# Block attention and a routed expert layer on one core: the first unit's weight loads move to another queue, v is loaded six tiles ahead

## The chip, the cores and the metric

The kernel runs on one core of a Trainium2 chip. The metric is the device time of one execution in microseconds (us). TensorE does the matrix products and transposes, VectorE (DVE), ScalarE (ACT) and GpSimd (POOL) the element-wise work; SyncE (SP) only issues transfers (DMAs). GpSimd issues transfers too, on a queue of its own. All transfers are carried by the same 16 DMA engines.

## What is computed

Attention in blocks of 64 tokens, without any link between blocks, and then a layer of 16 experts in 4 groups, of which each token uses one:

```
# q, k, v: batch 8, heads 8, 576 tokens, 64 wide; blocks of 64 tokens
attn = softmax(q_c @ k_c^T / 8)          # 64 x 64 for each block and head
x = attn @ v_c                           # seen as 4608 tokens x 512
g = argmax(x @ w_group)                  # one of 4 groups
e = argmax(x @ w_expert[g])              # one of its 4 experts
out[token] = p(g) * p(e) * relu(x @ w1[g, e]) @ w2[g, e]
# w1: 16 x 512 x 1024, w2: 16 x 1024 x 512, all float32
```

## The kernel before

The 4608 tokens are 36 tiles of 128 (two blocks of 64 with all 8 heads). A first stage does attention and routing tile by tile; rows of x go to a buffer in HBM (`xs`), sorted by expert. A second stage, the critical block with loops at run time, takes units of up to 256 rows of one expert through w1 and w2. The change lies in the first stage.

**Order.** The order of TensorE, VectorE and ScalarE in the first stage is written out by hand; SyncE and GpSimd are not named in that clause. `HEAD` runs first, then one round for each t from 0 to 32, then `TAIL`, a long list for the last tiles. A word is a letter and a number: `Qn` (`load_qk`) loads q and k for two tiles, four transfers of 256 KB or more and smaller ones; `Vn` (`load_v`) loads v for one tile, 256 KB; `an` transposes q (even n) or k (odd n) of tile n // 2 on TensorE, with a copy on ScalarE; `b` is the scores of a tile (L277), `s` subtracts the maximum on VectorE, `e` the exponential on ScalarE, `c` transposes the probabilities on TensorE and copies them (`pT`) on ScalarE, `p` is the product with v (L313), `n` normalizes into x on VectorE (L330), `x` transposes x (TensorE, and a copy on ScalarE). Round t holds, in this order:

```
b(t) s(t) p(t-2) n(t-2)   a(2t+6)   c(t-1) e(t)   a(2t+7)   Q(t//2+4) if t is even   x(t-3)   load_v(t+4)   EXTRA[t]
```

`FIRST` stands in the place of the first `a` of round 0. After every four tiles the logits of that group of tiles are formed (`1`, L349, which reads the router's weights), transposed back (`2`) and ranked (`3`); VectorE's routing steps are spread between its other work by `more()`.

**Extras.** `EXTRA` puts further steps at the end of a round. `G0` (`load_wg`, L572) loads the router's weights, five small transfers by SyncE. `Z0` to `Z4` (`prefill`, L582) write zeros into parts of `xs` by SyncE. `F0` to `F5` (`first_loads`, L523) are for the first unit, whose expert `e0` VectorE chooses after 16 tiles: `F0` reads the number into a register and loads the first half of w1 (1 MB), `F1` the second half, `F2` and `F3` gather the unit's 256 rows, `F4` and `F5` load the halves of w2. Before, all of them are issued by GpSimd. `P0` to `P7` (`prep_static`, L192) split w1 into a high part (a copy on ScalarE, L197) and the rest (a subtraction on GpSimd, L198); P0, P1, P4 and P5 read the first half, the others the second. `X0` and `X1` (`first_x`) transpose the gathered rows. In `TAIL`, `W` copies w2's high part (L559, the first one shortly after the scores of tile 33), and `L` (`first_l1`) starts the first unit's first product. `R0` and `R1` load the next expert's w1 by SyncE into the same two buffers.

**Buffers.** The raw q and k have three buffers, v has eight (`NV`), the transposes share four PSUM tiles on their way to ScalarE. x of a group of four tiles has three buffers (`xl` and two of `xpool`); a buffer is written again when the rows of the group three before have been scattered to `xs` (L483, GpSimd). The scatter also waits for the zeros of `prefill`, which lie in the same buffer in HBM.

Of the kernel before, what the change touches and what calls it, by code (L numbers as in the profile page):

```python
# [27 lines left out]
E = G * EG  # L28
NT = N // P
# [11 lines left out]
NB0, NL0 = 2, 3  # L41
PB = 1

HEAD = "Q0 V0 Q1 V1 Q2 V2 V3 a0 a1"
FIRST = "a2 a3 Q3 a4 a5 a6"
EXTRA = {2: "G0", 4: "Z0", 5: "Z1", 6: "Z2", 7: "Z3", 8: "Z4",
         24: "F0", 26: "F1", 27: "F2 F3 P0", 28: "P1 P2", 29: "P3", 30: "P4 P5 F4", 31: "P6 X0", 32: "P7 X1 F5"}
TAIL = ("c32 m1 b33 m1 36 m1 s33 p31 b34 e33 W1 m4 x30 m1 n31 m3 s34 m1 L0 m1 e34 L1 c33 x31 b35 17 l7 m2"
# [43 lines left out]
def moe_kernel(tc, q, k, v, w_group, w_expert, w1, w2, cst, out):  # L92
    nc = tc.nc
    w1 = w1.rearrange("g e d f -> (g e) d f")
    w2 = w2.rearrange("g e f d -> (g e) f d")
    with ExitStack() as ctx:
# [24 lines left out]
        e0 = wpool.tile([1, 1], I32, name="e0")  # L121
# [22 lines left out]
        NP = 2  # L144
# [31 lines left out]
        def load1(eng, e, j):  # L176
            s = w1[e] if isinstance(e, int) else w1[ds(e, 1)].rearrange("o a b -> (o a) b")
            return eng.dma_start(w1r[j], s.rearrange("(c p) f -> p c f", p=P)[:, K1 * j:K1 * j + K1])

        def load2(eng, e, j):  # L180
            s = w2[e] if isinstance(e, int) else w2[ds(e, 1)].rearrange("o a b -> (o a) b")
            return eng.dma_start(w2r[j], s.rearrange("(c p) f -> p c f", p=P)[:, K2 * j:K2 * j + K2])
# [17 lines left out]
        with ExitStack() as c1:  # L200
# [24 lines left out]
            st, TL, FAST = {}, NT - 1, GL - 1  # L225

            def spans(c0, n):
                out, c = [], c0
                while c < c0 + n:
                    b, j = divmod(c, NCH)  # L230
                    m = min(c0 + n - c, NCH - j)
                    out.append((c - c0, m, b, j))
                    c += m
                return out
# [10 lines left out]
            def load_v(t):  # L245

                va = vbufs[t % NV]
                for i, m, b, j in spans(2 * t, 2):
                    nc.sync.dma_start(va[i * CH:(i + m) * CH, :, 0:HD], v[b, :, j * CH:(j + m) * CH, :].rearrange("h s d -> s h d"))
                st[t] = dict(va=va)  # L250
# [271 lines left out]

            def first_loads(i):  # L523
                if i == 0:
                    st["e0"] = nc.values_load(e0[0:1, 0:1], engines=[nc.gpsimd.engine], min_val=0, max_val=E - 1,
                                              skip_runtime_bounds_check_because=WHY)
                if i < NP:
                    load1(nc.gpsimd, st["e0"], i)
                elif i < NP + 2:
                    j = i - NP  # L530
                    r = nc.values_load(xi0[0:1, j:j + 1], engines=[nc.gpsimd.engine], min_val=0, max_val=E * RE * P,
                                       skip_runtime_bounds_check_because=WHY)
                    nc.gpsimd.dma_start(xg0[:, j, :], xs[ds(r, P), :])
                else:
                    load2(nc.gpsimd, st["e0"], i - NP - 2)

            def first_x(j):
                pt = ps_t.tile([P, 4, P], F32, name="tp")
# [27 lines left out]
            def more(n=1):  # L566

                for _ in range(n):
                    while routing and next(routing[0], True):
                        routing.pop(0)  # L570
# [8 lines left out]
            def last(t):  # L579
                return t >= 0 and t % NG == NG - 1  # L580
# [8 lines left out]
            def run(seq):  # L589
                g = dict(P=prep_static, X=first_x, L=first_l1, H=first_hi, D=first_lo, W=prep2_hi, w=prep2_lo, y=lambda i: prep2_lo(i, nc.vector), F=first_loads, R=reload, V=load_v,  # L590
                         Q=load_qk, G=load_wg, Z=prefill, a=stage_a)
                f = dict(b=stage_b, s=stage_sub, c=stage_ct, e=stage_exp, p=stage_pv, n=stage_norm, x=stage_xt)
                for z in seq.split():
                    if z[0] == "m":
                        more(int(z[1:]))
                    elif z[0] in g:
                        g[z[0]](int(z[1:]))
                    elif z[0] == "1":
                        stage_e1(int(z[1:]))
                    elif z[0] == "l":  # L600
                        stage_lts(int(z[1:]))
                    elif z[0] == "2":
                        stage_e2(int(z[1:]))
                    elif z[0] == "3":
                        stage_e3(int(z[1:]))
                    elif 0 <= int(z[1:]) < NT:
                        f[z[0]](int(z[1:]))

            with tc.manual_schedule(engines={mybir.EngineType.PE, mybir.EngineType.DVE, mybir.EngineType.Activation}):
                nc.sync.dma_start(cs[:, P:], cst[:, P:])  # L610
                run(HEAD)
                for t in range(TL - 2):
                    run("b%d s%d p%d n%d" % (t, t, t - 2, t - 2))
                    if last(t - 4):
                        run("1%d" % ((t - 4) // NG))
                    run("a%d" % (2 * t + 6) if t else FIRST)
                    if last(t - 4):
                        run("l%d" % ((t - 4) // NG))
                    if last(t - 7):
                        run("3%d" % ((t - 7) // NG))  # L620
                    more(2)
                    run("c%d e%d" % (t - 1, t))
                    run("a%d" % (2 * t + 7))
                    if t % 2 == 0 and t <= 26:
                        run("Q%d" % (t // 2 + 4))
                    run("x%d" % (t - 3))
                    if t + 4 < NT:
                        load_v(t + 4)
                    if last(t - 4):
                        run("2%d" % ((t - 4) // NG))  # L630
                    run(EXTRA.get(t, ""))
                run(TAIL)
# [751 lines left out]
```

## Time and profile before

| | |
|---|---|
| median of 3 runs | 685.59 us (681.66 to 689.75) |
| the profiled execution | 684.17 us |
| its span, from the first to the last instruction | 682.5 us |
| TensorE busy | 628.1 us (92%) |
| VectorE, ScalarE, GpSimd busy | 369.3, 293.3, 147.7 us |
| moved by DMA | 128.10 MB, 188 GB/s over the span |
| first stage | up to about 219 us |

The profile shows the profiled execution alone. Times in its views are counted from the first instruction. An engine counts as busy while it works, not while it waits for a semaphore; the "idle" of a row is the time just before its instructions, with what ended it behind the arrow. Line numbers (L277) are those of the kernel before. A DMA row by SPq or POOLq is the issue, not the transfer; the time to landing stands apart.

### The profile page before, as it was taken

Reading aid. Unit: us, or ns where it says so; the run is one execution under the profiler, and the core shown is the slowest. Engines: PE = TensorE matmul, PEld = TensorE weight load, DVE = VectorE, ACT = ScalarE, POOL = GpSimd, SP = SyncE. Lnnn points to the kernel's source line nnn. Section 1 sums busy time; section 2 is a strip of 40 time slices with the busy share of each in tenths; the row PEclk is TensorE's granted clock in tenths of the full one; section 3 lists DMA queues with packets and bytes.
Section 4 is the critical chain, followed back from the end, with each engine's and each line's share of the span. In section 5 each row is a group of like instructions: output and inputs, shape, how many; then the busy total and the mean of one; then the engine's idle time right before and its main releaser. Section 6 shows DMA issues by size and latency. Waiting matters only on the chain.

```text
span 682.5 us, 16774 instructions
## 1 busy us (share of the span) xinstructions
PE 628.1 (92%) x5866; PEld 558.9 (82%) x5867; DVE 369.3 (54%) x695; ACT 293.3 (43%) x418; POOL 147.7 (22%) x217
## 2 busy tenths in 40 slices
PE   5979789989587979999999999999999999999992
PEld 4868778877576778998988989998999998998981
DVE  1447566747458646722457776472721777854210
ACT  3545545657344243511438545251611465552110
POOL 1000222226325322022122411222111214222110
PEclk9889989989798979999999999999999999999996
DMA  9999999999932496831176984554441656931010
GB/s 190 208 174 213 246 222 236 221 257 261 263 122 79 150 370 234 300 121 59 57 260 212 335 331 176 168 207 139 165 151 61 259 218 235 335 129 64 21 45 15
DMA packets 151634, 128.10 MB, mean 188 GB/s; under 512 B 119006, under 2 KB 119262, under 8 KB 151584
## 3 DMA queue, kind: packets, MB, share of 16 engines
q1 hardware_dynamic: 140720, 93.76, 50.0%
q0 software_dynamic: 10864, 33.64, 14.1%
q8 instruction: 35, 0.57, 0.4%
q14 instruction: 15, 0.12, 0.1%
HBM read 106.23 MB, written 21.93 MB: 188 GB/s over the span
## 4 chain that ended last, share of the span: by engine, by line
PE 84%; issue 3%; DMA 3%; SPq 3%; DVE 3%; ACT 1%; POOLq 0%; DVEq 0%; ACTq 0%
PE py L827 27%; PE ph L812 18%; PE lgk L812 6%; PE ph L796 5%; PE o L313 5%; PE sc L277 5%; PE tp L259 5%; SPq L243 2%; PE tp L300 2%; PE tp L342 2%; DMA va<-in_v_dram 2%; PE py L844 2%; PE pxt L712 2%; PE lgk L349 1%; PE ph L758 1%
## 5 line engine op out<-in xcount | busy, mean ns | idle before, releaser
L812 PE MATMUL ph<-xt,w1h 128*128 128x256 f32 x672 | 100.4, 286 | 5.4 <-issue 5.4
L812 PEld LDWEIGHTS ph<-xt,w1h 128*128 128x128 f32 x672 | 91.0, 195 | 6.9 <-issue 5.9
L967 ACT ACTIVATE hth<-ph 128x512 fp32r<-128x512 f32 x43 | 25.7, 598 | 153.8 <-PE ph L812 150.6
L1295 POOL DMA_INDIRECT out_dram<-xl,io x37 | 41.6, 1124 | 166.2 <-DVE xl L1028 153.4
L1042 DVE TENSOR_TENSOR w2l<-w2r,w2h 128x1024 fp32r<-128x1024 f32 x60 | 69.5, 1218 | 6.5 <-ACT w2h L982 5.0
L1038 DVE TENSOR_TENSOR w1l<-w1r,w1h 128x2048 fp32r<-128x2048 f32 x28 | 63.0, 2289 | 13.2 <-ACT w1h L954 11.6
L827 PE MATMUL py<-w2h,hth 128*128 128x512 f32 x264 | 67.7, 398 | 0.0
L827 PE MATMUL py<-w2l,hth 128*128 128x512 f32 x264 | 65.3, 390 | 0.0
L827 PE MATMUL py<-w2h,htl 128*128 128x512 f32 x264 | 65.2, 389 | 0.0
L1028 DVE TENSOR_SCALAR xl<-py,io 128x512 f32<-128x512 f32 x33 | 24.7, 748 | 68.3 <-PE py L827 68.3
L285 DVE TENSOR_REDUCE m<-sc 128x8 f32<-128x512 f32 x36 | 24.8, 688 | 66.2 <-PE sc L277 66.1
L1061 DVE SCALAR_TENSOR_TENSOR htl<-ph,hth 128x512 fp32r<-128x512 f32 x40 | 27.4, 688 | 58.6 <-ACT hth L967 58.2
L827 PEld LDWEIGHTS py<-w2l,hth 128*128 128x128 f32 x264 | 49.6, 188 | 10.6
L827 PEld LDWEIGHTS py<-w2h,htl 128*128 128x128 f32 x264 | 49.6, 188 | 10.3
L259 PE MATMUL tp<-cs,qk 128*128 128x128 f32 x288 | 49.7, 302 | 8.1 <-DMA qk<-in_q_dram 6.9
L313 PE MATMUL o<-va,pT 64*64 64x65 f32 x1152 | 42.5, 225 | 14.8 <-DMA va<-in_v_dram 6.7
L827 PEld LDWEIGHTS py<-w2h,hth 128*128 128x128 f32 x264 | 47.6, 188 | 10.2 <-ACT hth L1013 0.9
L812 PE MATMUL ph<-xt,w1l 128*128 128x256 f32 x336 | 55.1, 286 | 0.5 <-DVE w1l L1038 0.5
L954 ACT CAST w1h<-w1r 128x2048 fp32r<-128x2048 f32 x28 | 52.2, 1905 | 4.1 <-DMA w1r<-in_moe_w_dram 2.1
L313 PEld LDWEIGHTS o<-va,pT 64*64 64x64 f32 x1152 | 39.0, 141 | 16.6 <-issue 13.5
L958 ACT CAST w2h<-w2r 128x2048 fp32r<-128x2048 f32 x28 | 52.3, 1928 | 0.0
L259 PEld LDWEIGHTS tp<-cs,qk 128*128 128x128 f32 x288 | 35.4, 153 | 18.6 <-issue 15.0
(259 smaller groups left out, 1057.5 us busy)
## 6 DMA issues: line engine op xcount, KB each, us to landing
w1r<-in_moe_w_dram SPq DMA_DIRECT2D x30, 1024.0 KB, 5.7
w2r<-in_moe_w_dram SPq DMA_DIRECT2D x30, 1024.0 KB, 7.3
xgr<-xs POOLq DMA_DIRECT2D x38, 257.0 KB, 5.6
qk<-in_q_dram SPq DMA_DIRECT2D x32, 256.0 KB, 5.5
qk<-in_k_dram SPq DMA_DIRECT2D x32, 256.0 KB, 5.8
va<-in_v_dram SPq DMA_DIRECT2D x32, 256.0 KB, 5.7
w1r<-in_moe_w_dram POOLq DMA_DIRECT2D x2, 1024.0 KB, 10.6
w2r<-in_moe_w_dram POOLq DMA_DIRECT2D x2, 1024.0 KB, 8.3
```

Source lines behind the costliest of these rows:

```text
L259: nc.tensor.transpose(pt[:, hp, :], st["q", t // 2][:, t % 2, z, 2 * hp:2 * hp + 2].rearrange("p h d -> p (h d)"), ident)
L277: nc.tensor.matmul(sc[HALF[x], hp, c], lhsT=st["T", u, 0][HALF[x], hp, k0:k0 + CH], rhs=st["T", u, 1][HALF[x], hp, k0:k0 + CH], start=True ...
L313: nc.tensor.matmul(o[HALF[c], x, hp * W:hp * W + W], lhsT=pT[HALF[c], hp, HALF[x]], rhs=s["va"][HALF[c], 2 * hp + x], start=True, stop=True)
L796: m = pe.matmul(ph[n], a_[:, c, 0:P], w_[:, c, n * 512:(n + 1) * 512], start=(i == 0), stop=(i == 11))
L812: m = pe.matmul(ph[f // 2][:, f % 2 * 256:f % 2 * 256 + 256], w_[:, c, f * P:(f + 1) * P], a_[:, c, :], start=(i == 0), stop=(i == 11))
L827: m = pe.matmul(py[j], a_[:, f, half[j]], w_(b, f), start=(i == 0), stop=(i == 23))
L954: lambda b, s, j: ac.copy(wt[b][0][:, s], w1r[j]), K1)
L958: lambda b, s, j: ac.copy(wt[b][2 + j], w2r[j]), K2)
L1038: lambda b, s, j: ve.tensor_sub(wt[b][1][:, s], w1r[j], wt[b][0][:, s].bitcast(F32)), K1, js)
L1042: m = ve.tensor_sub(wt[b][4 + 2 * j + i], w2r[j][:, 2 * i:2 * i + 2], wt[b][2 + j][:, 2 * i:2 * i + 2].bitcast(F32))
L1061: ve.scalar_tensor_tensor(out=htl()[:, 2 * b:2 * b + 2, :], in0=ph[b].rearrange("p (f t) -> p f t", f=2), scalar=0.0, in1=hth()[:, 2 * b:2 ...
L1295: gp.indirect_dma_start(out, bass.IndirectOffsetOnAxis(ap=io[:, j, 0:1].bitcast(I32), axis=0), yb[:, j, :], None, bounds_check=N - 1, oob_ ...
```

## The change

The loads of the first unit's w1 and w2 (`F0`, `F1`, `F4`, `F5`) are issued by SyncE, and SyncE reads `e0`; the gathers `F2` and `F3` stay with GpSimd. `F0` moves from round 24 to 26, `F1` from 26 to 27, `F5` from 32 to 31; `F2` and `F3` stay in round 27 and `F4` in round 30. `P0` to `P6` stand one round later than before, `P7` stays in round 32, `X0` and `X1` stay in rounds 31 and 32. v is loaded six tiles ahead of the round in place of four: `V3` leaves `HEAD`, `V3`, `V4` and `V5` enter `FIRST`, and each round loads v(t+6). `G0` moves from round 2 to round 1.

```diff
--- before.py
+++ after.py
@@ -41,10 +41,10 @@
 NB0, NL0 = 2, 3
 PB = 1
 
-HEAD = "Q0 V0 Q1 V1 Q2 V2 V3 a0 a1"
-FIRST = "a2 a3 Q3 a4 a5 a6"
-EXTRA = {2: "G0", 4: "Z0", 5: "Z1", 6: "Z2", 7: "Z3", 8: "Z4",
-         24: "F0", 26: "F1", 27: "F2 F3 P0", 28: "P1 P2", 29: "P3", 30: "P4 P5 F4", 31: "P6 X0", 32: "P7 X1 F5"}
+HEAD = "Q0 V0 Q1 V1 Q2 V2 a0 a1"
+FIRST = "a2 a3 Q3 V3 a4 V4 a5 V5 a6"
+EXTRA = {1: "G0", 4: "Z0", 5: "Z1", 6: "Z2", 7: "Z3", 8: "Z4",
+         26: "F0", 27: "F1 F2 F3", 28: "P0", 29: "P1 P2", 30: "P3 F4", 31: "P4 P5 X0 F5", 32: "P6 X1 P7"}
 TAIL = ("c32 m1 b33 m1 36 m1 s33 p31 b34 e33 W1 m4 x30 m1 n31 m3 s34 m1 L0 m1 e34 L1 c33 x31 b35 17 l7 m2"
         " p32 m2 s35 e35 c34 n32 27 m1 p33 m3 W2 c35 m1 p34 n33 W0 n34 m1 x32 W4 p35 m1 x34 x33 m4 n35 m3 x35"
         " m3 R1 m3 y0 H0 m1 W3 m1 37 18 l8 y1 m2 L2 m1 y2 m1 D0 m2 y3 m1 W7 W6 y4 m4 28 m6 L3 m5 W5 y5 H1 m2 L4"
@@ -522,17 +522,17 @@
 
             def first_loads(i):
                 if i == 0:
-                    st["e0"] = nc.values_load(e0[0:1, 0:1], engines=[nc.gpsimd.engine], min_val=0, max_val=E - 1,
+                    st["e0"] = nc.values_load(e0[0:1, 0:1], engines=[nc.sync.engine], min_val=0, max_val=E - 1,
                                               skip_runtime_bounds_check_because=WHY)
                 if i < NP:
-                    load1(nc.gpsimd, st["e0"], i)
+                    load1(nc.sync, st["e0"], i)
                 elif i < NP + 2:
                     j = i - NP
                     r = nc.values_load(xi0[0:1, j:j + 1], engines=[nc.gpsimd.engine], min_val=0, max_val=E * RE * P,
                                        skip_runtime_bounds_check_because=WHY)
                     nc.gpsimd.dma_start(xg0[:, j, :], xs[ds(r, P), :])
                 else:
-                    load2(nc.gpsimd, st["e0"], i - NP - 2)
+                    load2(nc.sync, st["e0"], i - NP - 2)
 
             def first_x(j):
                 pt = ps_t.tile([P, 4, P], F32, name="tp")
@@ -624,8 +624,8 @@
                     if t % 2 == 0 and t <= 26:
                         run("Q%d" % (t // 2 + 4))
                     run("x%d" % (t - 3))
-                    if t + 4 < NT:
-                        load_v(t + 4)
+                    if t + 6 < NT:
+                        load_v(t + 6)
                     if last(t - 4):
                         run("2%d" % ((t - 4) // NG))
                     run(EXTRA.get(t, ""))
```

## Rows read from the trace of the kernel before

**Rows 1.** The page: busy time of each engine (share of the span) and instructions.

```profile
PE 628.1 (92%) x5866; PEld 558.9 (82%) x5867; DVE 369.3 (54%) x695; ACT 293.3 (43%) x418; POOL 147.7 (22%) x217
```

**Rows 2.** Windows by stage: length, busy time by engine, TensorE's clock, DMA share, GB/s.

```profile
80.00:130.00 50.00, 43.05 (x768) 36.71 (x766) 28.83 (x105) 25.67 (x52) 10.76 (x15) 0.93 1.06 227
130.00:180.00 50.00, 41.39 (x739) 35.37 (x738) 28.97 (x92) 27.71 (x56) 23.74 (x26) 0.93 1.08 269
180.00:220.00 40.00, 32.81 (x441) 28.69 (x441) 26.01 (x85) 18.78 (x36) 12.62 (x13) 0.93 0.36 121
```

**Rows 3.** Waits of SyncE's queue, 0 to 181 us: total, times, longest.

```profile
SPq L243 <- PE sc L277: 3.0, 4, 1.0
```

**Rows 4.** Waits of TensorE, 20 to 181 us.

```profile
PE o L313 <- DMA va<-in_v_dram: 6.7, 2, 6.1
PE o L313 <- issue: 6.1, 1, 6.1
PE lgk L349 <- DMA wg<-in_moe_w_expert_dram: 3.6, 1, 3.6
```

**Rows 5.** The chain that ended last, 158 to 190 us: start, us, what.

```profile
164.06 13.66 DMA va<-in_v_dram
```

**Rows 6.** The page's DMA issues: count, size of one, median us to landing.

```profile
va<-in_v_dram SPq DMA_DIRECT2D x32, 256.0 KB, 5.7
```

**Rows 7.** TensorE in order of time, 156 to 216 us: start, us, instructions.

```profile
160.55 1.15 PE L313 MATMUL o<-va,pT 64*64 64x65 f32 x32 [0.53 <-DMA va<-in_v_dram]
...
170.57 1.15 PE L277 MATMUL sc<-kT,qT 64*64 64x64 f32 x32
177.85 2.00 PE L313 MATMUL o<-va,pT 64*64 64x65 f32 x32 [6.13 <-DMA va<-in_v_dram]
...
184.26 1.15 PE L277 MATMUL sc<-kT,qT 64*64 64x64 f32 x32
```

**Rows 8.** Windows of three stretches, columns as in rows 2.

```profile
100.00:110.00 10.00, 9.90 (x179) 8.44 (x179) 7.32 (x24) 5.60 (x12) 1.17 (x2) 1.00 0.94 204
...
176.90:183.70 6.80, 5.85 (x52) 5.76 (x53) 1.84 (x10) 2.39 (x5) 0.19 (x1) 0.50 0.95 217
250.00:255.00 5.00, 5.00 (x44) 5.00 (x44) 1.72 (x3) 3.29 (x3) 0.00 (x0) 1.00 1.05 396
```

**Rows 9.** SyncE's queue in order of time (four stretches): start, us of issuing, transfers.

```profile
69.80 1.04 SPq L584 DMA_DIRECT2D xs<-pad  x1
...
127.67 1.01 SPq L249 DMA_DIRECT2D va<-in_v_dram  x1
128.78 0.74 SPq L243 DMA_DIRECT2D qk<-in_q_dram  x1
...
164.06 16.64 SPq L249 DMA_DIRECT2D va<-in_v_dram  x7
...
167.38 5.60 SPq L249 DMA_DIRECT2D va<-in_v_dram  x2
```

**Rows 10.** GpSimd in order of time, with the issues of its transfers.

```profile
76.39 1.12 POOL L483 DMA_INDIRECT xs<-x,pos  x1 [71.78 <-DMA va<-in_v_dram]
...
133.01 0.79 POOL L178 DMA_DIRECT2D w1r<-in_moe_w_dram  x1
...
163.79 0.78 POOL L182 DMA_DIRECT2D w2r<-in_moe_w_dram  x1
164.58 1.32 POOL L198 TENSOR_TENSOR w1l<-w1r,w1h 128x512 fp32r<-128x512 f32 x1
```

**Rows 11.** ScalarE in order of time: copies of w1 and the first of w2.

```profile
152.04 0.66 ACT L197 CAST w1h<-w1r 128x512 fp32r<-128x512 f32 x1
...
157.13 1.17 ACT L197 CAST w1h<-w1r 128x512 fp32r<-128x512 f32 x2
...
188.34 0.60 ACT L559 CAST w2h<-w2r 128x512 fp32r<-128x512 f32 x1
```

**Rows 12.** VectorE in order of time: the first write into a used x buffer.

```profile
87.06 0.69 DVE L330 TENSOR_TENSOR x<-o,rc 128x512 f32<-128x512 f32 x1 [7.51 <-DMA xs<-x,pos]
```

**Rows 13.** Transfers into w1r: by SyncE (180 to 190 us), then by GpSimd (130 to 145 us).

```profile
DMA to landing us min/median/max: 4.8/5.9/6.9
DMA to landing us min/median/max: 9.4/10.6/11.8
```

## The prediction

> **What bounds the kernel now.** The engines' totals come first: TensorE is busy 92% of the span [rows 1], but that is a mean over two stages, and the change touches only the first. The windows by stage [rows 2] split them: from 80 to 180 us the DMA share stands at 1.06 and 1.08 while TensorE works 43.05 and 41.39 of 50 us; from 180 to 220 us the DMA share falls to 0.36. So I read the attention stage as bound by its transfers until the last v is in. The waits of SyncE's queue up to 181 us confirm it: the largest entry is 3.0 us in four waits [rows 3], and the seven entries add up to 10.8 us. The queue hardly waits for buffers; it hands out transfers as fast as the DMA engines take them, and each issue is held up by the transfers ahead of it. TensorE's own waits then show where a late transfer is met: 6.7 us for v, 6.1 us put down to "issue" (an x buffer, below), 3.6 us for the router's weights [rows 4]. The chain of waits gives the last gate: one v transfer (tile 30) took 13.66 us from issue to landing [rows 5], where 5.7 us is the median [rows 6]. TensorE's timeline shows what that does: scores of tile 32 at 170.57, then nothing until tile 30's value product at 177.85, and tile 33's scores at 184.26 [rows 7]. That last time, b33, is my yardstick: behind it the tail of the list and the routed stage run on as before, and what moves b33 moves the end.
>
> **The price of a transfer.** A 256 KB transfer of q, k or v costs 262144 B / 204 GB/s = 1.29 us, by the stretch 100 to 110 us, in which almost nothing else moves [rows 8]. From 128.78 us (Q15 is issued) to 167.38 + 5.60 = 172.98 us (v32 has been issued) [rows 9] the queue hands out Q15 to Q17 and v26 to v32, 12 + 7 = 19 such transfers, 24.4 of 44.2 us. The other 19.8 us went to GpSimd's queue beside it: four weight loads of 1 MB, the first issued at 133.01, the third at 163.79 [rows 10], two groups of scattered rows (2.1 MB) and two gathers (0.5 MB): 6.8 MB, or 345 GB/s. A weight load so costs 3.0 us of everybody's transfers; the ends are 2.65 (396 GB/s, 250 to 255 us [rows 8]) and 3.9 us (269 GB/s, 130 to 180 us [rows 2]).
>
> **The weights move to SyncE's queue.** At 128.78 the new order has handed out the same set as the old one (Q0 to Q14, v0 to v25). Up to the end of v32's issue it then has the same 19 transfers, 24.4 us, but beside them only scatter and gathers, 2.6 MB at 345 GB/s, 7.6 us: 160.8 us. Then comes F0. Its half of w1 lands behind the backlog: 5.7 us for a v [rows 6] and 3.0 - 1.3 us more for its size, at 168.2 us. F1 follows behind v33: 168.2 + 1.3 + 3.0 = 172.5 us. So w1, which now passes the backlog on a queue of its own, will stand in it.
>
> Who waits for that is ScalarE. Its order is written out, and P0, the first copy of w1, stands at the end of tile 28's round. In the old kernel P0 ran at 152.04, P1 and P2 at 157.13 [rows 11]; in the new one P0 is due at about 157 and can't start before 168.2. Queued behind it are the copies of the next round, tile 28's pT among them, and TensorE's value product of tile 28 needs that. TensorE can still run round 29 and the scores of tile 30, then it stands. After the landing: P0, one transpose's copy, pT, three copies at the 0.5 us step of [rows 11], so p28 at 169.8 us instead of 160.55 [rows 7]. From p28 to the point where p30 is due, the old kernel takes 170.57 + 1.15 - 160.55 = 11.2 us [rows 7]; from p30 to b33 it takes 6.4 us, of which 5.8 us lie in the stretch at half clock (0.50 from 176.9 to 183.7 [rows 8]), so 3.5 us at full clock. That gives 184.5. After TensorE's 10 us of idling I expect the half clock again and take the same loss of 2.9 us (ends 0 and 5.8): 187.4. From p28 on ScalarE now has nine copies of w1 and x to make where it had five; it is busy 27.7 of 50 us there [rows 2], so I take 0.8 of these 2 us (ends 0 and 2). b33 comes at 188.2 instead of 184.3: **+3.9 us**. P2 wants the second half, 172.5, and is due after that anyway.
>
> **v six tiles ahead, w2 behind the last v.** v30 no longer meets w2 (the loads at 163.79 and after) and stands in front of Q17; its 6.1 us of waiting go, which is counted above, since p30 follows b32 at once. What is late next is P0. w2 lands at 172.5 + 2.6 (v34, v35) + 3.0 = 178.1 and 181.1; its first copy ran at 188.34 [rows 11] and comes some 4 us later still. The cover is the 14 us between, and the DMA engines are nearly idle then, so this costs nothing; without the cover each us late would be a us. The buffer of v(t+6) frees with p(t-2) of the same round; the queue runs behind TensorE (v32, of round 28, was still being issued when TensorE had the scores of tile 32 behind it [rows 7, 9]), so this adds no wait. Each q and k load stands behind two more v, 2.6 us later; so does each pad.
>
> **The router's weights at tile 1.** They are issued about three transfers, 3.9 us, earlier, and the wait of 3.6 us goes [rows 4]. I give it nothing at the end: the next gate eats it. The first scatter starts at 76.39 [rows 10], just after the last pad landed, which was issued at 69.80 [rows 9] and now comes 2.6 us later. That scatter frees the x buffer for which VectorE waits 7.51 us, until 87.06 [rows 12]. So TensorE is 2.6 us late there instead of 3.6 early, and both vanish in the wait for P0. If that wait weren't there, the 2.6 us would show (ends -5 and +2.6).
>
> **What costs nothing.** SyncE reads the expert's number before F0: GpSimd issues on it at 133.01 [rows 10], SyncE gets there at 160.8. GpSimd is rid of four issues, work that nobody waits for.
>
> **Sum.** The profiled execution took 684.17 us (span 682.5 and 1.7 around it); + 3.9 is 688.1. The median of the three runs, 685.59, lies 1.4 above it: **689.5 us**, 0.6% more. A measurement of this kernel can tell about 1%, 6.9 us, from no change; the runs before spread over 8.1.
>
> **Rivals.** *A: w1 is not late.* Only TensorE, VectorE and ScalarE follow the written order; SyncE's may be chosen otherwise, with F0 ahead of Q17 or earlier. For it: on GpSimd the first w2 load came ahead of a w1 subtraction that stands before it in the program [rows 10]. Against it: SyncE's queue ran q, k, v and pads in program order, Q15 behind v25 and the seven last v behind Q17 [rows 9]. Then v30's 6.1 us and its 2.9 of half clock go and 0.8 on ScalarE comes: 8.2 less, 677.4 us.
>
> *B: the load does not stand in the backlog for so long.* In the old kernel a load of w1 by SyncE landed in 4.8 us and one by GpSimd in 11.8 [rows 13]. If 4.8 held at 160.8, P0 could start at 165.6, b33 would come 2.6 us sooner: +1.3, 686.9 us. Against it: the 4.8 us load was issued after the last v, with no backlog. The Trainium skill, page "DMA: Bandwidth & Descriptors", section "Issuing engine by pattern", gives simple loads to Sync and calls that path generally faster. By that rule B would be the outcome; here the trace has the shorter time only at an empty queue, and no run so far shows it at a full one.
>
> *C: SyncE's order sets F0 later, not earlier.* F0 waits for a register read, the v loads don't; if F0 falls behind v33 to v35, three transfers, w1 lands 3.9 us later and P0 with it: +7.8, 693.4 us. It decides from two transfers on, 2.6 us, which with the 3.9 reaches 1%. For it: nothing else hides P0's wait. Against it: the number is there 28 us before.
>
> **How the numbers follow.** Forecast 0.42, A 0.25, B 0.13, C 0.20. The forecast's own range, from the price of a load (its two ends shift w1 by -0.5 to +1.5 us), the clock (-2.9 to +2.9), ScalarE (-0.8 to +1.2) and the backlog (a v landed in 3.8 to 13.7 us, mostly near 5.7), is 685 to 694. With A's upper half and most of C the range that should hold 8 times in 10 is 677 to 695: about 0.12 lies below (half of A), 0.08 above (C with a dear load). Faster by over 1% means under 678.7: most of A, 0.18. Slower by over 1% means over 692.5: three quarters of C and the dear end of the forecast, 0.25. Within 1%: 0.57.
>
> **What would show it.** Right: in the profile after, TensorE has no wait for the router's weights near 46 us; the wait for the x buffer ends near 90 us; SyncE issues w1 near 161 us behind v32; ScalarE stands before its first w1 copy until about 168, and TensorE about 10 us before p28; no wait for v follows; b33 near 188. Wrong: w1 issued by SyncE before 155 us (A), landed within 5 us (B), or behind v35 (C). A stage 80 to 160 us that runs with a DMA share well below 1 would break the ground under all of it.

## The result, and the profile after

The changed kernel takes 693.48 us in the median of 20 runs (689.65 to 701.37), the kernel before 685.47 us in 20 (680.71 to 693.53). The medians differ by 8.0 us; the ratio is 1.0133, with a 95% interval of 1.0106 to 1.0159, so the change costs 1.3%. Each ratio in this document is taken over the executions that lie within 1.5% of the fastest of their kernel, so that it can differ from the quotient of the two medians, and the profiled execution of the changed kernel, 701.37 us (span 699.7), the longest of its 20, is not among them. Predicted were 689.5 us, 3.9 us more than before. Because that execution stands out, two further profiled executions of the same kernel are set beside it: e17 (691.77 us, span 690.1) and, further below, e12 (689.09 us, span 687.5).

The page's busy times, which answer to [rows 1]:

```profile
PE 635.6 (91%) x5866; PEld 565.7 (81%) x5867; DVE 370.1 (53%) x695; ACT 293.4 (42%) x418; POOL 144.4 (21%) x213
```

The windows of [rows 2] after the change (length, busy time by engine, clock, DMA share, GB/s):

```profile
80.00:130.00 50.00, 35.54 (x586) 30.81 (x586) 22.31 (x78) 19.30 (x40) 12.33 (x15) 0.83 1.04 226
130.00:180.00 50.00, 42.87 (x744) 37.30 (x742) 28.21 (x103) 24.68 (x50) 11.80 (x14) 0.91 0.98 228
180.00:220.00 40.00, 33.52 (x486) 28.96 (x484) 21.10 (x65) 20.18 (x40) 15.70 (x15) 0.86 0.46 160
```

TensorE, VectorE and ScalarE run as many instructions as before, GpSimd four fewer. TensorE works 35.54 us between 80 and 130 where it had worked 43.05 [rows 2], so it falls behind well ahead of the weights. The DMA share up to 180 us is still about 1 (1.04 and 0.98; 1.06 and 1.08 before).

The waits of SyncE's queue, 0 to 181 us (total, times, longest), three of the five entries at v:

```profile
SPq L249 <- PE sc L277: 6.9, 2, 3.8
SPq L249 <- PE tp L259: 3.3, 5, 1.2
...
SPq L249 <- PE tp L342: 2.0, 2, 1.5
```

L249 is the load of v. In [rows 3] the largest entry was 3.0 us in four waits at L243, the load of q and k, and all entries came to 10.8 us; the eleven of the changed kernel come to 24.2. The queue now stands at v until TensorE has freed a v buffer.

SyncE in order of time (start, us of issuing), with the first loads of w1 and the last of v:

```profile
160.71 0.94 SPq L249 DMA_DIRECT2D va<-in_v_dram  x1
162.88 1.59 SPq L178 DMA_DIRECT2D w1r<-in_moe_w_dram  x1
164.56 0.76 SPq L249 DMA_DIRECT2D va<-in_v_dram  x1
165.52 4.89 SPq L178 DMA_DIRECT2D w1r<-in_moe_w_dram  x1
170.51 4.47 SPq L249 DMA_DIRECT2D va<-in_v_dram  x2
```

F0 stands behind v32 and ahead of v33, as written and as forecast, at 162.88 in place of the forecast 160.8. ScalarE's copies of w1, which answer to [rows 11]:

```profile
174.99 0.62 ACT L197 CAST w1h<-w1r 128x512 fp32r<-128x512 f32 x1 [5.33 <-DMA w1r<-in_moe_w_dram]
177.94 0.65 ACT L197 CAST w1h<-w1r 128x512 fp32r<-128x512 f32 x1
180.27 0.62 ACT L197 CAST w1h<-w1r 128x512 fp32r<-128x512 f32 x1 [1.68 <-DMA w1r<-in_moe_w_dram]
```

P0 came at 152.04 before and comes at 174.99 now, because w1 is not there: 12 us from its issue. TensorE, which answers to [rows 7]:

```profile
161.27 1.14 PE L277 MATMUL sc<-kT,qT 64*64 64x64 f32 x30
...
176.63 2.00 PE L313 MATMUL o<-va,pT 64*64 64x65 f32 x32 [1.84 <-ACT pT L302]
...
197.25 1.15 PE L277 MATMUL sc<-kT,qT 64*64 64x64 f32 x32
```

The first row is b28 (the scores of tile 28), at 161.27 where it was at 151.05; then p28 (the value product of tile 28) at 176.63 (160.55), waiting for ScalarE's pT, which stands behind P0; the last is b33 at 197.25 (184.26). No wait for v is left in front of it. The wait of VectorE for the x buffer [rows 12] has grown, too:

```profile
92.55 0.69 DVE L330 TENSOR_TENSOR x<-o,rc 128x512 f32<-128x512 f32 x1 [13.74 <-DMA xs<-x,pos]
```

So the profile has two candidates: ScalarE before P0, and the queue that waits for v buffers with pads, q and k behind it.

**The second execution (e17).** ScalarE, then TensorE (b28, b30, p28, p30, b33), then SyncE:

```profile
171.98 0.62 ACT L197 CAST w1h<-w1r 128x512 fp32r<-128x512 f32 x1 [14.58 <-DMA w1r<-in_moe_w_dram]
...
151.18 1.15 PE L277 MATMUL sc<-kT,qT 64*64 64x64 f32 x32
...
159.01 1.15 PE L277 MATMUL sc<-kT,qT 64*64 64x64 f32 x32
173.62 2.00 PE L313 MATMUL o<-va,pT 64*64 64x65 f32 x32 [13.46 <-ACT pT L302]
...
185.16 1.10 PE L313 MATMUL o<-va,pT 64*64 64x65 f32 x32
192.54 1.97 PE L277 MATMUL sc<-kT,qT 64*64 64x64 f32 x32
...
163.45 1.34 SPq L178 DMA_DIRECT2D w1r<-in_moe_w_dram  x1
```

Here b28 is where it was before, and what follows is the forecast's picture: the scores of tile 30 run, TensorE stands for 13.46 us, ScalarE for 14.58. In the first execution, which has short stalls of TensorE (last section), b28 was 10 us late already, and the same late w1 showed as a wait of only 5.33 us. The length of that wait is therefore no measure of what w1's lateness costs; the times of p28 and b33 are a better one.

### The profile page after: what moved, and what is told of

Same layout as the page of the kernel before. It is cut to its first block, busy times and chain, and to the rows that moved or that the text cites. A ratio compares the mean times of both kernels' runs of the same rounds, so it can differ in the third digit from the quotient of the medians.

```text
span 699.7 us, 16788 instructions
## 1 busy us (share of the span) xinstructions
PE 635.6 (91%) x5866; PEld 565.7 (81%) x5867; DVE 370.1 (53%) x695; ACT 293.4 (42%) x418; POOL 144.4 (21%) x213
## 4 chain that ended last, share of the span: by engine, by line
PE 81%; issue 5%; DMA 4%; DVE 3%; SPq 3%; ACT 2%; POOLq 0%; DVEq 0%; another core or an unknown queue 0%; ACTq 0%
PE py L827 26%; PE ph L812 18%; PE lgk L812 6%; PE ph L796 5%; PE sc L277 4%; PE o L313 4%; PE tp L259 4%; DMA qk<-in_k_dram 2%; PE tp L342 2%; PE tp L300 2%; PE py L844 2%; PE pxt L712 2%; SPq L243 2%; PE ph L758 1%; PE py L781 1%
## 5 line engine op out<-in xcount | busy, mean ns | idle before, releaser
L313 PE MATMUL o<-va,pT 64*64 64x65 f32 x1152 | 45.2, 227 | 21.9 <-issue 17.6
L259 PE MATMUL tp<-cs,qk 128*128 128x128 f32 x288 | 51.1, 309 | 11.8 <-DMA qk<-in_q_dram 9.1
```

The lines of the kernel that those rows point to most:

```text
L259: nc.tensor.transpose(pt[:, hp, :], st["q", t // 2][:, t % 2, z, 2 * hp:2 * hp + 2].rearrange("p h d -> p (h d)"), ident)
L313: nc.tensor.matmul(o[HALF[c], x, hp * W:hp * W + W], lhsT=pT[HALF[c], hp, HALF[x]], rhs=s["va"][HALF[c], 2 * hp + x], start=True, stop=True)
```

## The experiments

Theory 1: the cost is ScalarE's wait for w1. Theory 2: it is v six tiles ahead; in the form 2a because SyncE stands at v(t+6) until p(t-2) has freed its buffer, in the form 2b because pads, q and k stand behind two more v in the order. Rows of one group (e1 to e4, e5 to e8, e9 to e12, e15 and e16, e17 and e18) ran together on one chip; "us" is the median, "before" that of the kernel before beside them.

| run | what | us | before | ratio, 95% |
|---|---|---|---|---|
| e1 | v six ahead alone | 694.44 | 684.40 | 1.0111 (1.0067 to 1.0155) |
| e2 | weights on SyncE alone | 688.44 | 684.40 | 1.0061 (1.0025 to 1.0098) |
| e3 | w2 alone, behind the last v | 684.08 | 684.40 | 1.0006 (0.9966 to 1.0045) |
| e4 | router's weights at tile 1 alone | 686.32 | 684.40 | 1.0007 (0.9963 to 1.0051) |
| e5 | e1 with ten v buffers | 678.45 | 680.73 | 0.9988 (0.9946 to 1.0030) |
| e6 | before with six v buffers | 679.37 | 680.73 | 0.9953 (0.9912 to 0.9995) |
| e7 | changed kernel, ten v buffers | 688.61 | 680.73 | 1.0110 (1.0067 to 1.0154) |
| e8 | changed kernel, v four ahead | 689.93 | 680.73 | 1.0130 (1.0087 to 1.0173) |
| e9 | changed kernel, F0 in round 24 | 691.58 | 684.83 | 1.0124 (1.0062 to 1.0186) |
| e10 | e1 again | 695.24 | 684.83 | 1.0187 (1.0114 to 1.0260) |
| e11 | e5 again | 685.87 | 684.83 | 1.0026 (0.9986 to 1.0066) |
| e12 | changed kernel again | 691.63 | 684.83 | 1.0128 (1.0064 to 1.0191) |
| e15 | changed kernel, F0 and F1 in round 24 | 684.54 | 687.14 | 0.9977 (0.9953 to 1.0001) |
| e16 | e1 with one more instruction | 688.59 | 687.14 | 0.9986 (0.9940 to 1.0032) |
| e17 | changed kernel, a third time | 694.11 | 686.51 | 1.0151 (1.0076 to 1.0227) |
| e18 | e15 again | 683.87 | 686.51 | 0.9988 (0.9951 to 1.0025) |

### One part at a time (e1 to e4)

**e1**, against before:

```diff
-HEAD = "Q0 V0 Q1 V1 Q2 V2 V3 a0 a1"
-FIRST = "a2 a3 Q3 a4 a5 a6"
+HEAD = "Q0 V0 Q1 V1 Q2 V2 a0 a1"
+FIRST = "a2 a3 Q3 V3 a4 V4 a5 V5 a6"
...
-                    if t + 4 < NT:
-                        load_v(t + 4)
+                    if t + 6 < NT:
+                        load_v(t + 6)
```

> Only v is loaded six tiles ahead; the weights stay on GpSimd's queue in their old rounds, the router's weights at tile 2. Theory 1 (the cost sits in ScalarE's wait for w1): w1 is in time, v30 stands ahead of Q17 and its 6 us wait goes, the pads come 2.6 us later: 678 to 685 us, and the wait for the x buffer grows from 7.5 to about 10 us. Theory 2 (the cost sits in v six ahead: pads, q and k come later, and the queue now waits for v buffers): slower by most of the 8 us, 690 to 694 us.

**e2**: F0, F1, F4 and F5 and the read of `e0` on SyncE, w1 and P0 to P7 in the rounds of the changed kernel, w2 behind v35:

```diff
-         24: "F0", 26: "F1", 27: "F2 F3 P0", 28: "P1 P2", 29: "P3", 30: "P4 P5 F4", 31: "P6 X0", 32: "P7 X1 F5"}
+         26: "F0", 27: "F1 F2 F3", 28: "P0", 29: "P1 P2", 30: "P3", 31: "P4 P5 X0 F4 F5", 32: "P6 X1 P7"}
...
-                    load1(nc.gpsimd, st["e0"], i)
+                    load1(nc.sync, st["e0"], i)
...
-                    load2(nc.gpsimd, st["e0"], i - NP - 2)
+                    load2(nc.sync, st["e0"], i - NP - 2)
```

> Only the first unit's weights move to SyncE's queue (w1 in rounds 26 and 27, w2 behind the last v, the w1 copies one round later); v stays four ahead, the router's weights at tile 2. Theory 1: w1 now stands behind v30 and not v32, so it lands 2.6 us earlier than in the full change; ScalarE still stands before its first copy of w1 for 6 us or more; 687 to 693 us. Theory 2: no slower than before, 679 to 686 us, since w2 no longer meets v.

**e3**: only w2 goes by SyncE, with a read of `e0` of its own there, in round 31 behind v35 (of the long line, the end that differs):

```diff
-30: "P4 P5 F4", 31: "P6 X0", 32: "P7 X1 F5"}
+30: "P4 P5", 31: "P6 X0 F4 F5", 32: "P7 X1"}
...
-                    load2(nc.gpsimd, st["e0"], i - NP - 2)
+                    load2(nc.sync, st["e0s"], i - NP - 2)
```

> Only w2 moves to SyncE's queue, behind the last v; w1 stays on GpSimd's in rounds 24 and 26. Both theories: v30 no longer meets w2, its 6.1 us wait and some half clock go: 676 to 681 us. Rival: the wait is only moved to q and k of the last tiles or to the chain of the tail, and the time stays at 684 to 687.

**e4**: only the router's weights move (of the line, the start that differs):

```diff
-EXTRA = {2: "G0",
+EXTRA = {1: "G0",
```

> Only the router's weights move to tile 1. Theory: the 3.6 us wait goes and the next gate, the x buffer that waits for the last pad and the first scatter, eats it: 684 to 687 us. Rival: the gain is kept to the end: 680 to 682 us.

The weights alone cost 0.6%, about the forecast 3.9 us. Whether by the mechanism of the forecast, e2's profile does not show: it is of the fastest of its twelve executions (683.32 us), ScalarE waits 3.0 us for w1 there, but TensorE stands only 0.40 us before p28, and b33 comes at 184.00, as before. w2 behind v and the router's weights cost and gain nothing; so the 676 to 681 us expected of e3 did not come at the median, though its profiled execution, the fastest of its twelve and without any wait for v, took 676.69. v six ahead alone was the dearest, 1.1%, which the sum had at no cost: for a while this made theory 2 the better one.

### Buffer or order (e5 to e8)

**e5** is e1, **e6** the kernel before, **e7** the changed kernel with another number of v buffers:

```diff
-NV = 8
+NV = 10
```

(e6: `NV = 6`, so that v(t+4) goes into the buffer that p(t-2) frees, in the old order of transfers). **e8** is the changed kernel with `HEAD`, `FIRST` and `load_v(t + 4)` of before.

> v six tiles ahead alone (+1.1% with eight v buffers), now with ten v buffers, so that v(t+6) goes into the buffer that p(t-4) freed, as v(t+4) does before. Theory 2a (SyncE stands at v(t+6) until p(t-2) of the same round has freed the buffer, and the q, k and pads queued behind it stand too): the waits of SyncE for TensorE's line of p and behind it shrink, 684 to 687 us, within 0.4% of before. Theory 2b (only the order: each q, k and pad stands behind two more v, 2.6 us, and the x buffer or the q is late by that): stays at 691 to 695 us, +0.9 to +1.5%.

> The kernel before with six v buffers in place of eight: the order of all transfers stays that of before, but v(t+4) now goes into the buffer that p(t-2) of the same round frees. Theory 2a (the wait for the buffer costs): 690 to 694 us, +0.8 to +1.4%, with b33 later by 5 us or more. Theory 2b (the order costs): within 0.4% of before, 683 to 687 us.

> The changed kernel with ten v buffers. Theory 2a: what is left is the wait for w1, which cost 0.6% alone: 687 to 690 us, +0.4 to +0.8%, with the first w1 copy still the late one. Theory 2b: no change against the changed kernel, 692 to 695 us, +1.1 to +1.5%.

> The changed kernel with v four tiles ahead again: the weights on SyncE's queue and the router's weights at tile 1 are left. Theories 2a and 2b both say 687 to 690 us (+0.4 to +0.8%, what the weights cost alone). A theory in which the weights cost only together with v six ahead says 684 to 686 us, and one in which v six ahead hides part of the weights' wait says 691 us or more.

e5 speaks against 2b: the order of e1 with two more buffers costs nothing. e6 speaks against 2a: SyncE stands 13.3 us for v buffers there and the kernel is no slower. Its waits at L249, 0 to 181 us:

```profile
SPq L249 <- PE tp L300: 4.4, 1, 4.4
SPq L249 <- PE tp L259: 4.0, 4, 1.7
SPq L249 <- PE sc L277: 1.9, 1, 1.9
SPq L249 <- PE tp L342: 1.6, 2, 1.4
SPq L249 <- PE o L313: 1.4, 3, 0.7
```

And e7 and e8 keep the whole cost of the change without v in eight buffers six ahead. What both have in common with the changed kernel, beside the router's weights and w2, which cost nothing by themselves, is the late P0; ScalarE and SyncE, first in e8, then in e7:

```profile
169.10 0.62 ACT L197 CAST w1h<-w1r 128x512 fp32r<-128x512 f32 x1 [13.12 <-DMA w1r<-in_moe_w_dram]
...
160.02 0.93 SPq L178 DMA_DIRECT2D w1r<-in_moe_w_dram  x1
```

```profile
169.25 0.62 ACT L197 CAST w1h<-w1r 128x512 fp32r<-128x512 f32 x1 [12.02 <-DMA w1r<-in_moe_w_dram]
...
161.55 0.90 SPq L178 DMA_DIRECT2D w1r<-in_moe_w_dram  x1
```

Theory 2 falls as an account of the changed kernel. With v four ahead F0 is issued at 160.02 (forecast 160.8) and P0 starts at 169.10 (168.2). One thing stays open: e8 costs 1.3% and e2 0.6%, though they differ only in the router's weights and in w2's first half, which e8 issues ahead of v35; the two intervals just meet (1.0087 and 1.0098).

### w1 earlier, and e1 once more (e9 to e12)

**e9**, against the changed kernel:

```diff
-         26: "F0", 27: "F1 F2 F3", 28: "P0",
+         24: "F0", 26: "F1", 27: "F2 F3", 28: "P0",
```

> The changed kernel with its first w1 load two rounds earlier in SyncE's order (round 24, ahead of v31, Q17 and v32, six transfers or 7.7 us) and the second one round earlier; all else as changed. Theory 1 (the cost is ScalarE's wait for w1, 12 to 13 us at P0 in the two runs of the changed order that had no stalls of TensorE between): F0 issued near 153 to 155 us, w1 landed near 162, P0's wait 4 to 6 us, and the time 683 to 688 us where the changed kernel takes 689 to 694 (6 to 8 us less). Theory 2 (what costs is v six ahead in eight buffers): 1 us less at most.

**e10** is e1, **e11** is e5, **e12** the changed kernel, unaltered.

> v six ahead alone with eight v buffers, a second time, now beside the same with ten buffers on one chip. Theory 2a (the wait for the v buffer): 1.0 to 1.2% above before again and 0.8% or more above the one with ten buffers. Rival (the +1.1% came with the 18 short stalls of TensorE before the value products, which the run on the other chip didn't have): if these stalls are missing here, within 0.4% of before and of the one with ten buffers.

> v six ahead with ten v buffers, a second time. Theory 2a: within 0.4% of before, as the first time (0.9988). Rival (the short stalls decide): the same distance to before as with eight buffers, whichever it is.

> The changed kernel beside the others on this chip. Theory 1 alone: 689 to 692 us, +1.0 to +1.3%, with P0's wait of 10 us or more if TensorE has no short stalls between, and 3 to 7 us with them; theory 2a: 0.4% or more above the changed kernel with ten buffers (1.011), so 1.015 or more.

e9 brought nothing at the median. ScalarE shows why theory 1 need not fall for it:

```profile
165.20 0.65 ACT L197 CAST w1h<-w1r 128x512 fp32r<-128x512 f32 x1
168.20 0.64 ACT L197 CAST w1h<-w1r 128x512 fp32r<-128x512 f32 x1
173.62 0.62 ACT L197 CAST w1h<-w1r 128x512 fp32r<-128x512 f32 x1 [4.78 <-DMA w1r<-in_moe_w_dram]
```

P0 no longer waits, but P2, which reads the second half, does: F1, in round 26 behind v32, was issued at 166.20. The wait went from one half to the other, and that asked for both halves early. It is not the whole of e9's loss in this execution, its slowest (697.35 us): b33 came at 189.66, and from there to the first product of the routed stage it took 42.2 us where the kernel before took 35.0, with a granted clock of 0.52 from 190 to 200 us. Whether the late second half caused that, too, is not shown.

e12 came out as theory 1 had it, in the time and in P0's wait (3.65 us beside short stalls). SyncE, ScalarE, then TensorE (p28, b33):

```profile
160.18 0.56 SPq L178 DMA_DIRECT2D w1r<-in_moe_w_dram  x1
...
169.73 0.62 ACT L197 CAST w1h<-w1r 128x512 fp32r<-128x512 f32 x1 [3.65 <-DMA w1r<-in_moe_w_dram]
...
171.37 1.15 PE L313 MATMUL o<-va,pT 64*64 64x65 f32 x32 [1.28 <-ACT pT L302]
...
188.85 1.15 PE L277 MATMUL sc<-kT,qT 64*64 64x64 f32 x32
```

e10 and e11 by themselves are what 2a expects, and against its rival: e11 had 20 of the short stalls and stayed at 1.0026.

### Both halves early, the kernel before again, e1 with another layout (e13 to e16)

**e13** and **e14** are the kernel before, one profiled execution each (688.04 and 684.26 us). **e15**, against the changed kernel:

```diff
-         26: "F0", 27: "F1 F2 F3", 28: "P0",
+         24: "F0 F1", 27: "F2 F3", 28: "P0",
```

**e16** is e1 with a memset more on GpSimd at the start:

```diff
+            spare = cpool.tile([P, 1], F32, name="spare")
+            nc.gpsimd.memset(spare, 1.0)
             vbufs = []
```

> The kernel before, one more profiled execution. If the wait for v30 (6.1 us) and the half clock behind it are there in every execution, the prediction's credit of 8.2 us was right and the cost of the wait for w1 was put too low by the missing 4 us. If the wait is missing in this one or the next, with b33 at 180 to 182 us in place of 184.3, the credit was a feature of the execution that was profiled.

> The kernel before once more: as for the look ahead of it; the time of each of the two looks goes with the wait for v30, 4 to 8 us more where it is there.

> The changed kernel with both loads of w1 in round 24 of SyncE's order, ahead of v31, Q17 and v32. Theory 1 (ScalarE's wait for w1, in either half, is what costs): both halves land by 168 us, the waits at P0 and P2 together fall to 5 us or less, and the time is 3 to 7 us under the changed kernel's, +0.2 to +0.8% over before. Rival (the wait only moves, to q of tile 34 or v31 behind the two loads, or the cost lies in the x buffer's wait): +1.0 to +1.3% again.

> v six ahead alone with eight buffers, and one more instruction on GpSimd at the start (a memset of 128 by 1 that nobody reads). Theory 2a (the queue's wait for the v buffer): +1.1 to +1.9% as the two times before. Rival (those runs lost 3 to 6 us in the routed stage at one unit whose gather came 4 us late, by where the program's instructions lie): within 0.6% of before, and a routed stage of 459 to 464 us in place of 466 and 469.

e15 takes the whole cost away, though P0 still waits 5.42 us. The two further executions of the kernel before show that the wait for v30 is no constant: first e13 (p30, then b33), then e14 (p28, p30, b33):

```profile
183.53 2.00 PE L313 MATMUL o<-va,pT 64*64 64x65 f32 x32 [10.80 <-DMA va<-in_v_dram]
189.22 1.15 PE L277 MATMUL sc<-kT,qT 64*64 64x64 f32 x32
```

```profile
167.05 2.00 PE L313 MATMUL o<-va,pT 64*64 64x65 f32 x32 [4.60 <-DVE x L330]
...
179.67 1.15 PE L313 MATMUL o<-va,pT 64*64 64x65 f32 x32 [1.19 <-DMA va<-in_v_dram]
185.15 1.15 PE L277 MATMUL sc<-kT,qT 64*64 64x64 f32 x32
```

10.80 us in one, 1.19 in the other, 6.13 in [rows 7]; in e14 a wait of 4.60 us before p28 took its place and b33 came at 185.15 all the same. Neither b33 lay at the 180 to 182 us that the expectation gave for an execution without the wait. e16 was not slower than before, though by its profile it still lost time in the routed stage (last section); e1's cost is thus not a steady one.

### The two beside each other (e17, e18)

**e17** is the changed kernel, **e18** is e15, in one comparison.

> The changed kernel beside the one with both w1 loads early, on one chip. Theory 1 (ScalarE's wait for w1 is the cost): +0.9 to +1.4% over before, as the two times before.

> Both w1 loads in round 24 of SyncE's order, a second time. Theory 1: 6 to 10 us (0.9 to 1.5%) under the changed kernel of the same call, and within 0.4% of before. Rival (the first result, 0.9977, was the session's): within 0.4% of the changed kernel.

694.11 against 683.87 us: two words moved in SyncE's order, 10.2 us between the medians, and the changed kernel is back at before (0.9988). e18 by its profile: SyncE, ScalarE, TensorE (p28, then b33):

```profile
154.80 4.06 SPq L178 DMA_DIRECT2D w1r<-in_moe_w_dram  x2
...
164.95 0.62 ACT L197 CAST w1h<-w1r 128x512 fp32r<-128x512 f32 x1 [6.06 <-DMA w1r<-in_moe_w_dram]
...
166.59 1.96 PE L313 MATMUL o<-va,pT 64*64 64x65 f32 x32 [3.92 <-ACT pT L302]
...
185.28 1.98 PE L277 MATMUL sc<-kT,qT 64*64 64x64 f32 x32
```

Against e17, P0 is 7.0 us earlier, p28 7.0, b33 7.3, the end of the span 7.8 (682.3 against 690.1). e18 keeps v six ahead in eight buffers, the router's weights at tile 1, w2 behind v and the long wait for the x buffer: none of these costs anything that can be measured there. Theory 1 is shown as far as w1's place in SyncE's order is the cause. The way from there, over P0 and pT to p28, is read from the traces, in which all of them move by 7 us; no run moved P0 alone.

## Why the prediction was wrong

**What bounds the kernel**: right. The DMA share between 80 and 160 us stayed at about 1 (1.06 in e17, 1.06 before), and b33 carries the end to within some us: behind it lie 498.2 us before, and 497.6, 498.7 and 502.4 in e17, e12 and the first execution of the changed kernel.

**The mechanism**: right. w1 stands in the backlog behind v32, ScalarE stands at P0, TensorE at p28 after the scores of tile 30, and no wait for v follows. e18 shows that nothing of the cost is left at the end once w1 comes earlier; p28 is still 6.0 us later than before there, and b33 1.0, since p28 to b33 takes 18.7 us in place of 23.7.

**The step that failed is the size of two terms of the sum for b33.** The first is w1's landing, "lands behind the backlog ... at 168.2 us". P0 starts with it, and it came later in all three executions of the changed kernel:

| | F0 issued | from there to P0 | P0 | p28 | b33 |
|---|---|---|---|---|---|
| predicted | 160.8 | 7.4 | 168.2 | 169.8 | 188.2 |
| e12 | 160.18 | 9.6 | 169.73 | 171.37 | 188.85 |
| e17 | 163.45 | 8.5 | 171.98 | 173.62 | 192.54 |
| first execution | 162.88 | 12.1 | 174.99 | 176.63 | 197.25 |

The sum for the profiled executions goes, e17 against before:

- p28: 173.62 against 160.55, 13.1 later; the prediction had 169.8, 9.25 later.
- p28 to b33: 18.9 us; the prediction had 18.4, before 23.7 [rows 7].
- b33 to the end: 497.6 against 498.2.

That makes 7.6 us, which is the difference of the spans (690.1 and 682.5), against 3.9 predicted; the missing 3.7 are w1's landing, 3.8 late. The price from issue to P0 was too low each time. Why F0 itself was issued 2.65 us late here is not shown. The sentence "so this adds no wait" was wrong: SyncE waits at v 1.1 us before, and in e17 11.1 us in four entries:

```profile
SPq L249 <- PE tp L300: 4.4, 3, 2.3
...
SPq L249 <- PE tp L342: 3.5, 3, 1.7
...
SPq L249 <- PE lgk L457: 2.0, 1, 2.0
SPq L249 <- PE sc L277: 1.2, 1, 1.2
```

I had argued that the queue runs behind TensorE by more than a round; that was read at v32, at the end of the backlog, and with v six ahead it doesn't hold earlier. But the same program in e12 waits 13.9 us at v and issues F0 at 160.18, so these waits do not by themselves make F0 late.

**The second term is the credit for v30's wait** (6.1 us and 2.9 of half clock, by which p28 to b33 shrinks from 23.7 to 18.4). It fits the pair of e17 and the profiled execution before, but it was taken from an execution in which the wait happened to be 6.1; others had 10.80 and 1.19. In the medians, taking the wait away alone gained nothing (e3, 1.0006; its interval leaves at most 2.3 us). And e7 and e8, with P0 only 1 us behind the forecast time, still cost 7.9 and 9.2 us against 680.73. That points to the credit as the larger miss in the median, and e17 to the landing; the kernel before was not profiled beside e7 and e8, so how the two share the missing 4.1 us is left open. That e12 lies at the forecast in both b33 and time (688.1 predicted for an execution like the profiled one, 689.09 measured) is luck as far as the terms go: its landing was late too, its p28 to b33 shorter than predicted (17.5), and its group's median is 691.63.

**The pads, q and k**: the size was wrong, the conclusion right. The wait for the x buffer ended at 92.55 (91.60 in e17), not near 90, after 13.74 us where it was 7.51 [rows 12]. In its shadow the granted clock stood at 0.50, 1.2 GHz, with TensorE nearly idle; e17, 82.00 to 95.70:

```profile
82.00:95.70 13.70, 3.31 (x40) 2.04 (x40) 3.51 (x9) 0.00 (x0) 3.88 (x6) 0.50 1.14 246
```

And yet b28 came at 151.18 (151.05 before): TensorE had caught up by then. It vanished not in the wait for P0, as I had it, but ahead of it; e18, with the same wait and a short P0, loses nothing.

**The router's weights, w2 behind v**: right, neither costs anything (e4, e3). **Rivals**: A is false, SyncE kept the written order. B is false: from F0's issue behind a full queue to P0 it took 7.7 us (e7) to 12.1, against the 4.8 us of [rows 13] behind an empty one. The Trainium skill's preference for Sync with simple loads ("DMA: Bandwidth & Descriptors", "Issuing engine by pattern") gave no gain here: GpSimd's two loads took 9.4 and 11.8 us by [rows 13], about what SyncE's took in the backlog, and the first was issued 30 us earlier (133.01 against 163.45 in e17), since that queue had no backlog to pass. C's order did not occur. That the median, 693.48, lies at C's price of 693.4 is a coincidence; I had given a landing late by 3.9 us no other cause than that order.

## What to carry to other kernels

- A load that moves to a queue with a backlog must be moved up in that queue's order by the length of the backlog; here two rounds for the first half and three for the second decided between 1.3% slower and no change. Moving only the first of two halves moves the wait to the second.
- A wait in the profile is read by the time of what stands behind it, not by its length: w1's lateness showed as a wait of 3.65, 5.33 and 14.58 us in three executions of one program, while p28 came 10.8, 16.1 and 13.1 us later than before.
- Before a stall's removal is credited, read a second execution: the same program had that stall at 1.19, 6.13 and 10.80 us.

## What the runs showed of the hardware beside this

**Short stalls of TensorE that come and go with one and the same program.** e5 and e11 are one program; their waits of TensorE before the value products, e5 and then e11, 20 to 181 us:

```profile
PE o L313 <- issue: 5.3, 1, 5.3
```

```profile
PE o L313 <- issue: 8.9, 20, 0.7
```

The one of 5.3 us is the x buffer; the twenty are breaks of about 0.4 us inside a product's 32 matmuls, with nothing in the profile that ended them. All kernels profiled in the groups e1 to e4 and e9 to e12 had them, and the first execution of the changed kernel; those of e5 to e8 and of e13 to e18 did not. Beside them TensorE is late at b28: 157.20 in e12 and 161.27 in the first execution, 151.18 in e17. In the first execution the breaks of 96 to 161 us sum to only 3.5 us, so they are not the whole of its 10 us. e12 had made up for them by b33 (188.85, e17 192.54); whether they made the first execution the longest is not shown. Their cause is open.

**A late gather in the routed stage.** All three executions of v six ahead alone with eight buffers (e1, e10, e16) have a wait of TensorE that no other profile here has; e10, 300 to 500 us:

```profile
PE pxt L712 <- DMA xgr<-xs: 3.2, 2, 1.6
```

Counted from the first product of the routed stage (L852, moved by three lines in e3 and by two in e16) to the last instruction, they take 465.8, 469.2 and 467.2 us; the others take 459.1 to 463.9. Another layout (e16) did not remove it, and the changed kernel, with the same v order and buffers, does not have it. It may be a part of what e1 and e10 lost; that is not shown, since e16's median shows no loss, and the profile of e16 is of one of its longer executions (695.58 us). What v six ahead costs by itself stays open.

**The time to landing behind a full queue.** In e15 the two w1 loads, issued from 151.93 on, took 11.0 and 13.6 us to land: a load that is issued earlier into the backlog also stays in it longer, so 8.7 us of earlier issue gave 7.0 us of earlier P0 (e18 against e17).
